# Gate and value products by a 15-product scheme on three token blocks and three weight groups

## The chip, the cores and the metric

One core of a Trainium2 chip runs the whole program in one launch. The metric is device time in microseconds (us), the median of several runs.

## The reference, cut to what matters

Three parts follow one another. All is in float32 (the matrices of the two feed-forward parts come in as 64-bit floats).

```
attn = softmax within chunks of 64 tokens, 8 heads of 64, 8 x 576 tokens   -> x: 4608 x 512
h    = relu(x @ w_in)           w_in 512 x 2048
y    = (h * h) @ w_out          w_out 2048 x 512          -> y: 4608 x 512
gate = sigmoid(y @ w_gate)      w_gate 512 x 1536
val  = y @ w_val                w_val  512 x 1536
out  = (gate * val) @ w2_out    w2_out 1536 x 512
```

The change concerns `gate` and `val`.

## The kernel before, in words

Everything is kept transposed: 128 features on the partitions, tokens along the row. A float32 operand is split into a high and a low part (`split`: ScalarE writes the high part, VectorE subtracts it and writes the low part), and each 128x128 by 128x512 product is three matmuls on TensorE, high by high, low by high, high by low. So one block product over 256 input features is six matmuls.

Four stages follow each other on TensorE. Stage 1 is attention and `x @ w_in`. Stage 2 is `(h*h) @ w_out` (class `Long`, matmuls at L1097). Stage 3 is gate and val (class `Unit`, matmuls at L689). Stage 4 is the last product (class `Long` again). Each of these products uses the Winograd form of Strassen's scheme: a 2 by 2 arrangement of blocks, seven block products in place of eight. In stage 3 the input features make two halves, the weight rows two halves (twelve groups of 128 features, six pairs) and the tokens a pair of blocks of 512. There are nine token blocks, so four pairs, and block 0 is done alone as two halves of 256 columns. A unit is one pair of weight groups of one matrix by one pair of token blocks.

The token blocks of a unit need seven operands, four of them sums (`token_ops`: four subtractions of two blocks each on GpSimd, and fourteen splits). The results need three copies out of PSUM on ScalarE and three additions on VectorE. Then the gate takes four sigmoids on ScalarE, and val four multiplications, three on GpSimd and one on VectorE (`finish2`). The products are stored in DRAM (`ud`) for stage 4.

Weights are prepared during stages 2 and 3. `to_float32` turns a 64-bit block into float32: a load into `wr`, two passes on ScalarE (L526, L530), three on VectorE (L533, L537, L544), one on GpSimd (L551). `weight_group` makes of two such blocks four sums on GpSimd, and splits of 512, 512, 512 and 256 words (`wx`). `through_dram` stores these in DRAM, and before its first use in either half of the stage each weight operand is brought back once and stays in SBUF. Stage 3 goes twice over the tokens, with half of the weights each time.

The order on every engine is written out ahead of time by `Plan`: each operation is a job with a cost and a due time worked out backwards from the TensorE job that needs it. TensorE jobs of the `main` stream run in the order of the code. An engine takes the ready job that is due first, so preparation fills the gaps of VectorE. `look` bounds how long before its due time a job may take SBUF, and `lead` puts a load's due time earlier. The SBUF room is 206 KB a partition. In stage 1 the prepared weights of `w_in` hold eight times 14 KB of it, the token operands 42 KB and the attention output 12 KB. PSUM has eight banks of 128x512.

Of the kernel before, what the change touches and what calls it, by code (L numbers as in the profile page):

```python
# [36 lines left out]


# [336 lines left out]
def tile_attention_relu2_glu(  # L375
# [12 lines left out]
    nc = tc.nc  # L388
# [115 lines left out]
    turn, count = [], [0]  # L504

    def to_float32(src, name, look=None, raws=None):
# [8 lines left out]
        if src.shape[0] == DM:  # L515
            dma(
                lambda: at(raw, None, I32).rearrange("p (c x) -> p c x", c=KD),
                lambda: src.rearrange("(c p) f -> p c f", p=P),
                writes=[raw], size=P * BLK * 8, look=look,
            )  # L520
        else:
            dma(lambda: at(raw, None, I32), lambda: src, writes=[raw], size=P * BLK * 8, look=look)
# [656 lines left out]
    with tc.manual_schedule():  # L1179
# [106 lines left out]
        def blocks_g(s):  # L1286
            def load(r, c):
                got, n = [], W2[s]
                a = A2[s] + c * n
                for kp in range(G1):  # L1290
                    t = sbuf(n, "g")
                    f = r * G1 + kp
                    dma(lambda t=t: at(t), lambda f=f: gd[f][:, a:a + n],
                        [gb[f, b] for b in range(a // BL1, (a + n - 1) // BL1 + 1)], [t], size=P * n * 4, look=13.0)
                    got.append(t)
# [13 lines left out]
        def y_of(m, a, n):  # L1309
# [9 lines left out]
        halves = (range(G2 // 2), range(G2 // 2, G2))  # L1319
        order = [[*PAIRS[:2], (0,), *PAIRS[2:]], [*PAIRS[::-1], (0,)]]  # L1320
        LK = 260.0, 500.0
        back = {(m, g): prepared(w, g, G2, f"{'gv'[m]}{g}", LK[h is halves[1]])
                for h in halves for g in h for m, w in enumerate((wg, wv))}
        back_o = [prepared(w2o, f, G2, f"o{f}", 900.0, rows) for f in range(G2)]
        w2 = {}

        def tokens(s):
            blocks = {}
            for r, c in ((0, 0), (1, 0), (0, 1), (1, 1)):
                if len(s) == 1:  # L1330
                    t = sbuf(BLK, "yr")
                    dma(
                        lambda t=t: at(t).rearrange("p (k c) -> p k c", k=2),
                        lambda r=r, c=c: yd[:, 2 * r:2 * r + 2, c * HB:(c + 1) * HB],
                        y_of(2 * r, c * HB, HB) + y_of(2 * r + 1, c * HB, HB), [t], size=P * BLK * 4, look=30.0,
                    )
                    blocks[r, c] = [(t, 0)]
                    continue
                blocks[r, c] = []
                for kk in range(2):  # L1340
                    t = sbuf(BLK, "yr")
                    dma(
                        lambda t=t: at(t), lambda a=s[c] * BLK, m=2 * r + kk: yd[:, m, a:a + BLK],
                        y_of(2 * r + kk, s[c] * BLK, BLK), [t], size=P * BLK * 4, look=30.0,
                    )
                    blocks[r, c].append((t, 0))
            return token_ops(blocks, BLK)

        ub = {}
        gates = {}  # L1350

        def finish2(s, g, m):
            def finish(u, row, col, t):
                n, f = u.n, g + row * G2
                if m == 0:
                    src = t if t is not None else u.U
                    t = t if t is not None else sbuf(n, "s")
                    copy(u.words(t), [t], u.words(src), [src], n, func=ACTF.Sigmoid, soon=3.0)
                    gates[row, col] = t
                    return  # L1360
                gate = gates.pop((row, col))
                if t is None:
                    binary("DVE", u.words(gate), u.words(gate), u.words(u.U), ALU.mult, n, [gate], [gate, u.U])
                else:
                    binary("POOL", u.words(gate), u.words(t), u.words(gate), ALU.mult, n, [gate], [gate, t], soon=4.0)
                j = s[col] if len(s) == 2 else 0
                d = Buf(name="u")
                ub.setdefault((f, j), []).append(d)
                a = 0 if len(s) == 2 else col * HB
                dma(lambda: ud[f, j][:, a:a + n], lambda: at(gate), [gate], [d], size=P * n * 4, soon=6.0)  # L1370
            return finish

        def unit2(h, s, g, m):
            def make():
                more = None
                if state.get("s") != s:
                    (state["xs"], more), state["s"] = tokens(s), s
                if (m, g) not in w2:
                    w2[m, g] = {kind: load(look=50.0) for kind, load in back[m, g].items()}
                wide = len(s) == 2  # L1380
                return Unit(w2[m, g], state["xs"], BLK if wide else HB, per if wide else per_h,
                            finish2(s, g, m), f"{s}"), more
            return make

        seq = [(h, s, g) for h in range(2) for s in order[h] for g in halves[h]]
        p0, p1 = order[0][:2]
        seq[:6] = [(0, s, g) for s, g in ((p0, 0), (p1, 0), (p1, 1), (p0, 1), (p0, 2), (p1, 2))]
        units([unit2(h, s, g, m) for h, s, g in seq for m in range(2)])


# [3 lines left out]
        def last_blocks(s):  # L1394
            wide = len(s) == 2

            def load(r, c):
                out_ = []
                for kp in range(G2):
# [4 lines left out]
                        ub[f, j], [t], size=P * n * 4, look=30.0)  # L1404
# [90 lines left out]
```

## Time and profile before

| | |
|---|---|
| median of 3 runs | 1601.63 us (1601.32 to 1601.82) |
| the profiled execution, its own time | 1601.8 us |
| its span in the profile | 1600.0 us |
| TensorE busy | 1584.4 us, 99% of the span |
| VectorE, ScalarE, GpSimd busy | 1306.6, 972.0, 530.8 us |
| bytes moved | 333.27 MB, mean 208 GB/s |

The first lines of the profile's page say how much of the span each engine was busy; the chain says through which engine the last instruction was reached. PE is TensorE, PEld its weight load, DVE is VectorE, ACT ScalarE, POOL GpSimd, SP the engine that issues the transfers. The 1.8 us between time and span lie outside the profile's span. TensorE's granted clock is 1.00 of full speed in all slices.

### The profile page before, as it was taken

What the parts mean: (1) busy time and instruction counts of PE and PEld (TensorE: products, weight loads), DVE (VectorE), ACT (ScalarE), POOL (GpSimd) and SP (SyncE); (2) the same over time, 40 slices, a digit from 0 to 9 for tenths busy, and PEclk for the clock granted to TensorE, in tenths of its full rate; (3) what the DMA queues carried; (4) which work ended last, traced back from release to release, by engine and by line L of the source; (5) the groups of instructions that cost most, each with busy time, mean ns of one, the idle gap of its engine ahead of it and who ended that gap; (6) DMA issues with size and microseconds to landing.
All of it is one profiled execution on the core that took longest, in us unless ns stands there. A gap on an engine that the chain in (4) does not pass through costs nothing.

```text
span 1600.0 us, 29686 instructions
## 1 busy us (share of the span) xinstructions
PE 1584.4 (99%) x10209; PEld 1387.7 (87%) x10209; DVE 1306.6 (82%) x2170; ACT 972.0 (61%) x1922; POOL 530.8 (33%) x432
## 2 busy tenths in 40 slices
PE   8999999999999999999999999999999999999999
PEld 6998999999998888899888898888888888888888
DVE  6968878797989998999998797743786748889886
ACT  7986676676876656566665665543565545555554
POOL 2452402021442111111266685643576641000000
PEclk9999999999999999999999999999999999999999
DMA  9965667677884848487787547586447577866562
GB/s 214 275 166 143 155 190 187 175 207 218 267 290 148 276 152 261 155 280 241 255 279 267 183 146 244 186 281 217 168 162 245 196 260 257 250 196 164 150 174 52
DMA packets 381991, 333.27 MB, mean 208 GB/s; under 512 B 231824, under 2 KB 292240, under 8 KB 381840
## 3 DMA queue, kind: packets, MB, share of 16 engines
q1 hardware_dynamic: 381840, 331.38, 67.8%
q8 instruction: 80, 1.31, 0.4%
q14 instruction: 71, 0.58, 0.1%
HBM read 209.13 MB, written 122.16 MB: 207 GB/s over the span
## 4 chain that ended last, share of the span: by engine, by line
PE 92%; DVE 3%; ACT 2%; DMA 1%; SPq 1%; issue 1%; POOL 0%; DVEq 0%; ACTq 0%
PE bank L689 51%; PE bank L1097 37%; SPq L457 1%; PE bank L878 1%; PE bank L940 1%; PE bank L924 1%; PE bank L858 1%; DMA wraw__750<-in_moe_w_in_dram 0%; DMA wf<-wf__3185 0%; PE bank L1077 0%; DMA k__326<-in_k_dram 0%; DVE T__2019 L484 0%; DMA gd<-b__3834 0%; DVE B__760 L484 0%; DMA ql__4671<-in_q_dram 0%
## 5 line engine op out<-in xcount | busy, mean ns | idle before, releaser
L551 POOL TENSOR_TENSOR wf__6958<-wf__6958,wr__6912 128x512 int32<-128x512 int32 x18 | 28.2, 1568 | 163.1 <-DVE wf__6958 L544 119.8
L551 POOL TENSOR_TENSOR wf__3185<-wf__3185,wr__3118 128x512 int32<-128x512 int32 x16 | 21.8, 1361 | 174.0 <-DVE wf__3185 L544 120.1
L551 POOL TENSOR_TENSOR wf__7071<-wf__7071,wr__6912 128x512 int32<-128x512 int32 x18 | 25.4, 1413 | 99.0 <-DVE wf__7071 L544 73.2
L493 POOL TENSOR_TENSOR raw__523<-raw__724,raw__523 128x384 f32<-128x384 f32 x20 | 24.2, 1229 | 30.1 <-DVE B__653 L484 12.3
L530 ACT ACTIVATE wr__6912<-wr__6912 128x512 int32<-128x512 uint32 x36 | 23.9, 665 | 0.0
L484 DVE TENSOR_TENSOR wx__7016<-ws__7143,wx__7016 128x512 fp32r<-128x512 f32 x18 | 17.8, 988 | 6.0 <-ACT wx__7016 L479 6.0
L493 POOL TENSOR_TENSOR ws__7143<-wf__7071 128x256 f32<-128x256 f32 x12 | 12.5, 1038 | 30.5 <-DVE wx__7684 L484 29.9
L484 DVE TENSOR_TENSOR wx__7684<-ws__7143,wx__7684 128x512 fp32r<-128x512 f32 x18 | 17.9, 997 | 4.7 <-ACT wx__7684 L479 4.7
L484 DVE TENSOR_TENSOR wx__7154<-wf__7071,wx__7154 128x256 fp32r<-128x256 f32 x18 | 14.2, 787 | 3.5 <-ACT wx__7154 L479 3.5
L479 ACT ACTIVATE wx__7154<-wf__7071 128x256 fp32r<-128x256 f32 x18 | 7.4, 411 | 15.8 <-POOL wf__7071 L551 15.6
L493 POOL TENSOR_TENSOR ws__7143<-ws__7143,wf__6958 128x256 f32<-128x256 f32 x18 | 16.2, 898 | 1.2
L533 DVE TENSOR_SCALAR wf__7071<-wf__7071 128x512 f32<-128x512 f32 x18 | 11.8, 653 | 5.6 <-ACT wf__7071 L526 5.4
L533 DVE TENSOR_SCALAR wf__6958<-wf__6958 128x512 f32<-128x512 f32 x18 | 10.3, 572 | 6.3 <-ACT wf__6958 L526 6.3
L493 POOL TENSOR_TENSOR ws__7143<-wf__6958,wf__7071 128x256 f32<-128x256 f32 x18 | 15.3, 848 | 0.3
L526 ACT ACTIVATE wf__3185<-wr__3118 128x512 f32<-128x512 f32 x16 | 10.6, 664 | 6.9 <-DMA wf<-wf__3185 6.9
L904 DVE TENSOR_REDUCE mx__379<-bank 128x4 f32<-128x256 f32 x16 | 6.6, 415 | 10.0 <-PE bank L878 10.0
L526 ACT ACTIVATE wf__7071<-wr__6912 128x512 f32<-128x512 f32 x18 | 11.9, 662 | 4.4 <-DMA wr__6912<-in_moe_w_gate_dram 1.9
L544 DVE SCALAR_TENSOR_TENSOR wf__6958<-wr__6912,wf__6958 128x512 int32<-128x512 int32 x18 | 14.1, 781 | 0.2
L533 DVE TENSOR_SCALAR wf__3185<-wf__3185 128x512 f32<-128x512 f32 x16 | 8.1, 506 | 7.5 <-ACT wf__3185 L526 7.5
L544 DVE SCALAR_TENSOR_TENSOR wf__7071<-wr__6912,wf__7071 128x512 int32<-128x512 int32 x18 | 13.8, 766 | 0.3
L526 ACT ACTIVATE wf__6958<-wr__6912 128x512 f32<-128x512 f32 x18 | 11.9, 659 | 3.1 <-DVE wod__6685 L484 1.5
L904 DVE TENSOR_REDUCE mx__2010<-bank 128x4 f32<-128x256 f32 x16 | 6.7, 417 | 8.5 <-PE bank L878 8.5
(5753 smaller groups left out, 6044.5 us busy)
## 6 DMA issues: line engine op xcount, KB each, us to landing
ad<-wx__7016 SPq DMA_DIRECT2D x27, 512.0 KB, 4.1
ad<-wx__7684 SPq DMA_DIRECT2D x27, 512.0 KB, 5.1
wr__3118<-in_moe_w_out_dram SPq DMA_DIRECT2D x16, 512.0 KB, 4.6
wr__6912<-in_moe_w_gate_dram SPq DMA_DIRECT2D x12, 512.0 KB, 4.7
wr__6912<-in_moe_w_val_dram SPq DMA_DIRECT2D x12, 512.0 KB, 4.4
wr__6912<-in_moe_w_out_dram SPq DMA_DIRECT2D x12, 512.0 KB, 3.9
ad<-wx__7154 SPq DMA_DIRECT2D x18, 256.0 KB, 3.7
wf<-wf__3185 SPq DMA_DIRECT2D x16, 256.0 KB, 4.5
```

Source lines behind the costliest of these rows:

```text
L457: nc.sync.dma_start(out=a, in_=b)
L484: lambda: nc.vector.tensor_tensor(out=lo(), in0=at(src, n, F32, off), in1=hi().bitcast(F32), op=ALU.subtract),
L493: eng, cost(eng, n), lambda: e.tensor_tensor(out=o(), in0=a(), in1=b(), op=op),
L526: nc.scalar.activation(out=at(w), in_=t[:, :, 1].bitcast(F32), func=ACTF.Abs)
L530: nc.scalar.activation(out=low, in_=low.bitcast(U32), func=ACTF.Copy, scale=2.0**-29)
L533: nc.vector.tensor_scalar_max(at(w), at(w), TINY)
L544: nc.vector.scalar_tensor_tensor(out=wi, in0=words()[:, :, 1], scalar=-0x40000000, in1=wi, op0=ALU.bitwise_and, op1=ALU.bitwise_or,)
L551: nc.gpsimd.tensor_tensor(out=wi, in0=wi, in1=words()[:, :, 0], op=ALU.add)
L689: nc.tensor.matmul(out=o, lhsT=at(op, P, F32R, wi * size + half * HB + kk * P), rhs=at(xb, n, F32R, xi * xsize + off), start=(first and kk ...
L858: nc.tensor.transpose(out=at(ps, P, F32, hp * P), in_=at(r, P, F32, hp * P), identity=ident)
L878: nc.tensor.matmul(out=o[c][to, hp, :], lhsT=qv[part, hp, tok], rhs=kv[part, hp, tok], start=True, stop=True,)
L1097: nc.tensor.matmul(out=at(ps[m], n), lhsT=at(w, P, F32R, wi * size + half * HB + m * P), rhs=at(x, n, F32R, xi * n), start=(first and kp = ...
```

## The change

- Gate and val use a scheme of 15 block products for a 3 by 2 by 3 arrangement (18 in the plain form): three token blocks of 512 (`THREES`), two halves of the input features, three weight groups of 128 rows (`g`, `g + 4`, `g + 8`). There are three passes over the weights, one for each three token blocks, with four `Group3` in a pass.
- `STEPS` gives the order of the 15 products, the PSUM bank each goes to, and what is done to the banks after it. Gate and val run in step: each product is done for the gate and then for val.
- All sums move to VectorE: 11 token sums (`LEFT_SUMS`), 12 weight sums (`RIGHT_SUMS`), 11 additions of a bank for each matrix, and all nine multiplications of gate by val. GpSimd keeps the last step of `to_float32`, and the sums for `w2_out`.
- The token operands of a three (30 of 4 KB) stay in SBUF for a pass. The weights don't: each product loads its operand, gate and val beside each other (`w3`, 512 KB), from DRAM (`wd3`), so each is loaded in all three passes.
- The buffers of the preparation (26 KB) are taken in one piece by the first load, which has a lead of 260 us and a look of 500. The preparation of `w2_out` follows in the same load buffers, with look 300 and lead 200.
- Many transfers count for 0.7 of their bytes in the planner's own costs. The instructions of stages 1, 2 and 4 stay the same, but for their order.

```
 STEPS = [                 # product, bank, first in the bank, what follows ('c' copy, 'a' add a bank, 'f' finish)
    (13, 2, True, [('c', 'x1', 2, 1)]),
    (6, 0, True, [('a', 'x1', 'x1', 1, 0, -1), ('f', 'o6', 's', 'x1', 1, 0)]),
    (11, 5, True, [('c', 'x2', 5, 1), ('c', 'x3', 5, -1)]),
    (1, 0, False, [('a', 'x2', 'x2', 1, 0, -1)]),
    (3, 0, False, [('a', 'x3', 'x3', 1, 0, 1), ('f', 'o4', 's', 'x3', 1, 0)]),
    (7, 1, True, [('c', 'x4', 1, 1)]),
    (9, 3, True, [('a', 'x2', 'x2', 1, 3, -1), ('f', 'o3', 's', 'x2', 1, 0), ('c', 'x5', 3, -1)]),
    (0, 1, False, [('c', 'x6', 1, -1)]),
    (10, 3, False, [('a', 'x6', 'x6', 1, 3, -1), ('f', 'o2', 's', 'x6', 1, 1)]),
    (14, 1, False, [('a', 'x5', 'x5', 1, 1, -1), ('f', 'o5', 's', 'x5', 1, 0)]),
    (4, 2, False, [('c', 'x7', 2, 1)]),
    (8, 4, True, [('a', 'x6', 'x6', 1, 4, 1)]),
    (12, 2, False, [('a', 'x4', 'x4', 1, 2, -1), ('f', 'o0', 's', 'x4', 1, 0), ('a', 'x6', 'x6', 1, 2, 1), ('f', 'o1', 's', 'x6', 1, 0)]),
    (5, 4, False, [('a', 'x7', 'x7', 1, 4, 1)]),
    (2, 0, False, [('f', 'o7', 'b', 0, 1), ('a', 'x7', 'x7', 1, 0, 1), ('f', 'o8', 's', 'x7', 1, 0)]),
 ]
...
+        def weights3(g, m):
+            src = (wg, wv)[m]
+            have = {}
+            for c in range(3):
+                w = to_float32(columns(src, g + c * G3), f"w{m}", (500.0,500.0,500.0,500.0)[g], (raws3, chunks3))
+                for r in range(2):
+                    have[r * 3 + c] = (w, r * HB)
...
+            for p, *_ in STEPS:
+                v = RIGHT[p]
+                b, off = get(v)
+                op = ops3[0]
+                ops3.append(ops3.pop(0))
+                if p in TURNED:
+                    turned_split(op, b, off)
+                else:
+                    split(op, b, HB, off=off)
+                if sums.used(v) and v >= 6:
+                    free.append(b)
+                dma(lambda p=p: wd3[g, p][:, m * BLK:(m + 1) * BLK], lambda op=op: at(op, None, F32), [op], [wb3[g, p]],
+                    size=P * 8 * HB * 0.7, soon=8.0)
...
+        ahead[0] = 260.0
+        for g in range(G3):
+            for m in range(2):
+                weights3(g, m)
+        taken.extend([*raws2[2], *slots2[BLK], *slots2[HB]])
+        ahead[0] = 200.0
+        back_o = [prepared(w2o, f, G2, f"o{f}", 300.0, rows) for f in range(G2)]
...
+            def run(self):
+                for p, c, first, todo in STEPS:
+                    w = Buf(8 * BLK, name="w3", op=True)
+                    dma(lambda w=w: at(w, None, F32), lambda p=p: wd3[self.g, p], [wb3[self.g, p]], [w],
+                        size=P * 8 * BLK * 0.7, look=15.0)
+                    for m in range(2):
+                        if first:
+                            self.banks[m][c] = psum("M")
+                        product3(self.banks[m][c], w, m, self.xs[p], first)
+                        for step in todo:
+                            self.step(m, step)
...
+        for js in THREES:
+            xs = tokens3(js)
+            for g in range(G3):
+                Group3(js, g, xs).run()
```

## Rows read from the trace of the kernel before

**Rows 1.** The page: busy time of TensorE, and the chain by engine.

```profile
PE 1584.4 (99%) x10209; PEld 1387.7 (87%) x10209; DVE 1306.6 (82%) x2170; ACT 972.0 (61%) x1922; POOL 530.8 (33%) x432
...
PE 92%; DVE 3%; ACT 2%; DMA 1%; SPq 1%; issue 1%; POOL 0%; DVEq 0%; ACTq 0%
```

**Rows 2.** The chain in order of time: start, duration, what, matmuls.

```profile
474.02 345.06 PE bank L1097 x1680
819.08 513.27 PE bank L689 x2484
1337.02 254.44 PE bank L1097 x1224
```

**Rows 3.** Windows of all engines, stages 2 and 3: busy us (instructions), clock, DMA share, GB/s.

```profile
470.00:812.00 342.00, 342.00 (x1673) 290.63 (x1672) 324.56 (x546) 209.60 (x391) 59.66 (x48) 1.00 0.69 226
812.00:1330.00 518.00, 518.00 (x2498) 438.13 (x2497) 367.45 (x474) 283.35 (x534) 312.99 (x235) 1.00 0.63 216
```

**Rows 4.** Windows of all engines: 100 us in stage 2, 100 us in stage 3.

```profile
500.00:600.00 100.00, 100.00 (x443) 82.84 (x442) 97.80 (x157) 60.52 (x103) 11.60 (x8) 1.00 0.54 179
...
1000.00:1100.00 100.00, 100.00 (x443) 82.84 (x442) 52.82 (x75) 45.95 (x82) 48.51 (x39) 1.00 0.70 237
```

**Rows 5.** Windows of L689 where only products of 256 columns run: PE, PEld.

```profile
1310.00:1320.00 10.00, 10.00 (x86) 10.00 (x85) 1.00 0.79 264
1320.00:1330.00 10.00, 10.00 (x85) 10.00 (x85) 1.00 0.80 260
```

**Rows 6.** Timeline of VectorE, end of stage 2: start, duration, instruction.

```profile
776.79 0.68 DVE L484 TENSOR_TENSOR wx__7684<-ws__7143,wx__7684 128x512 fp32r<-128x512 f32 x1
777.39 0.41 DVE L484 TENSOR_TENSOR wx__7154<-wf__7071,wx__7154 128x256 fp32r<-128x256 f32 x1
777.73 0.68 DVE L484 TENSOR_TENSOR x__9212<-g__9227,x__9212 128x512 fp32r<-128x512 f32 x1
778.33 0.68 DVE L484 TENSOR_TENSOR wx__7016<-ws__7143,wx__7016 128x512 fp32r<-128x512 f32 x1
```

**Rows 7.** Groups of instructions by form, VectorE, 440 to 780: busy, mean ns, idle before.

```profile
L544 DVE SCALAR_TENSOR_TENSOR wf__6958<-wr__6912,wf__6958 128x512 int32<-128x512 int32 x6 | 4.1, 687 | 0.1
...
L537 DVE TENSOR_SCALAR wf__6958<-wf__6958 128x512 int32<-128x512 int32 x6 | 2.6, 426 | 0.1
L533 DVE TENSOR_SCALAR wf__7071<-wf__7071 128x512 f32<-128x512 f32 x6 | 2.5, 420 | 0.5 <-ACT wf__7071 L526 0.3
```

**Rows 8.** Windows of GpSimd's L551, stage 2.

```profile
470.00:812.00 342.00, 20.18 (x12) 1.00 0.69 226
```

**Rows 9.** Windows of GpSimd's L493, stage 3.

```profile
812.00:1330.00 518.00, 279.96 (x211) 1.00 0.63 216
```

**Rows 10.** The tile `wr`: its loads, ns min/median/max, first and last start.

```profile
L457 SPq DMA_DIRECT2D wr__6912<-in_moe_w_gate_dram x12: 383/384/483, 523.7 to 1030.0; - x12
L457 SPq DMA_DIRECT2D wr__6912<-in_moe_w_val_dram x12: 383/384/1512, 551.6 to 1055.0; - x12
```

**Rows 11.** Timeline of VectorE, start of stage 3: splits beside a GpSimd subtraction.

```profile
813.06 1.78 DVE L484 TENSOR_TENSOR B__9472<-yr__9336,B__9472 128x512 fp32r<-128x512 f32 x1
814.77 1.77 DVE L484 TENSOR_TENSOR B__9476<-yr__9345,B__9476 128x512 fp32r<-128x512 f32 x1
```

**Rows 12.** Timeline, stage 3: an addition from PSUM, and its wait on TensorE.

```profile
1068.42 0.69 DVE L493 TENSOR_TENSOR b__11795<-b__11795,bank 128x512 f32<-128x512 f32 x1 [0.21 <-PE bank L689]
```

**Rows 13.** Windows of all engines, start of stage 4; the last two numbers are DMA share, GB/s.

```profile
1345.00:1350.00 5.00, 5.00 (x23) 4.14 (x23) 4.93 (x9) 3.39 (x6) 0.00 (x0) 1.00 1.03 417
...
1360.00:1400.00 40.00, 40.00 (x178) 33.14 (x177) 32.53 (x53) 21.52 (x37) 0.00 (x0) 1.00 0.86 250
```

**Rows 14.** Windows of L1097, start of stage 4: the 10 us around the first of these.

```profile
1340.00:1350.00 10.00, 10.00 (x45) 8.28 (x45) 1.00 0.96 350
```

**Rows 15.** Groups of instructions, ScalarE, 812 to 1330.

```profile
L464 ACT ACTIVATE c__11380<-bank 128x512 f32<-128x512 f32 x7 | 4.2, 598 | 14.8 <-PE bank L689 14.8
```

**Rows 16.** The tile `ud`: a store, issue time in ns, first and last start.

```profile
L457 SPq DMA_DIRECT2D ud<-s__9956 x5: 319/319/320, 862.8 to 1006.6; - x5
```

More of the change, by code (lines that the diff above doesn't have):

```diff
@@ L502, in rows @@
         return w[f * P:(f + 1) * P, :]
-    turn, count = [], [0]
+    turn, count, taken, ahead = [], [0], [], [0.0]
     def to_float32(src, name, look=None, raws=None):
@@ new lines, in tile_attention_relu2_glu, with __init__, used @@
+        taken.extend([*raws3[1:], *chunks3, *sums3, *ops3])
+        steps_of = {id: (x, y, {"+": ALU.add, "-": ALU.subtract}[o]) for id, x, y, o in (*LEFT_SUMS,)}
+        sums_of = {id: (x, y, {"+": ALU.add, "-": ALU.subtract}[o]) for id, x, y, o in (*RIGHT_SUMS,)}
+        class Sums:
+            def __init__(self, of, wanted):
+                self.of, self.left = of, {}
+                for v in wanted:
+                    self.left[v] = self.left.get(v, 0) + 1
+                for x, y, _ in of.values():
+                    self.left[x] = self.left.get(x, 0) + 1
+                    self.left[y] = self.left.get(y, 0) + 1
+            def used(self, v):
+                self.left[v] -= 1
+                return not self.left[v]
@@ new lines, in tile_attention_relu2_glu, with product3, go @@
+        ub = {}
+        def product3(ps, w, m, xs, first):
+            def go():
+                o = at(ps, BLK)
+                for kk in range(2):
+                    for i, (wi, xi) in enumerate(((0, 0), (1, 0), (0, 1))):
+                        nc.tensor.matmul(
+                            out=o,
+                            lhsT=at(w, P, F32R, m * BLK + wi * HB + kk * P),
+                            rhs=at(xs[kk], BLK, F32R, xi * BLK),
+                            start=(first and kk == 0 and i == 0),
+                            stop=(kk == 1 and i == 2),
+                            skip_group_check=True,
+                        )
+            job("PE", 6 * per, go, [w, *xs] if first else [w, *xs, ps], [ps], stream="main")
@@ L1355, in finish @@
                 if m == 0:
[L1356 to L1359, printed above, removed]
+                    gate = sbuf(BLK, "s") if kind == "b" or left[0] else t
+                    copy(words(gate), [gate], words(t), [t], BLK, func=ACTF.Sigmoid, soon=3.0, scale=float(sign))
+                    self.gates[name] = gate
@@ L1367, in finish @@
+                f, j = self.g + c * G3, self.js[i]
                 d = Buf(name="u")
                 ub.setdefault((f, j), []).append(d)
[L1369 to L1388, printed above, removed]
+                dma(lambda: ud[f, j], lambda: at(gate), [gate], [d], size=P * BLK * 4 * 0.7, soon=6.0)
+        for js in THREES:
+            xs = tokens3(js)
+            for g in range(G3):
+                Group3(js, g, xs).run()
```

162 lines of the change are left out of this document (119 added, 43 removed), and 15 rows, old and new, of the table STEPS.

## The prediction

> **What bounds the kernel now.** I began with the page: TensorE is busy for 99% of the span, and 92% of the chain that ends last is TensorE's own [rows 1]. The chain in order of time then gives the stages: one unbroken piece of 345 us in stage 2, one of 513 us for gate and val, one of 254 us in stage 4 [rows 2]. No wait interrupts the stage that is changed. Its time is its count of matmuls, so any matmul that goes is time gained, as long as nothing else becomes late.
>
> What could become late is read from the windows. In stage 2 VectorE is busy for 324.6 of 342 us, in stage 3 for 367.5 of 518, the transfers take 0.69 and 0.63 of their engines [rows 3]. So the resource next to TensorE is VectorE, and it is fuller before the changed stage than in it. In a stretch of 100 us TensorE is held up by nothing with VectorE busy for 97.8 [rows 4]: I take that as the share that can be used.
>
> **Matmuls.** A matmul of 512 columns takes 100/443 = 0.2257 us [rows 4], one of 256 columns 20/171 = 0.117 us [rows 5]. Before: 4 pairs x 6 groups x 2 matrices x 7 products x 6 = 2016 wide ones and 6 x 2 x 42 = 504 narrow ones, 455.0 + 59.0 = 514.0 us (the chain shows 513.3 with some records missing [rows 2]). After: 3 passes x 4 groups x 2 x 15 x 6 = 2160 wide ones, 487.5 us. The change removes 26.5 us.
>
> **VectorE's price list.** Back to back, an operation of 512 words starts 0.60 us after the one before it, one of 256 words takes 0.34 (777.39 to 777.73) [rows 6], though the first is shown as 0.68 long. The three steps of a conversion are 0.42, 0.43 and 0.69 [rows 7], the last counted at its pitch of 0.60, so 1.45 us in all. Beside a GpSimd operation a split grew to 1.78 us [rows 11]. How much of that is usual comes from stage 2: 546 operations [rows 3], of which 12 conversions (12 on GpSimd [rows 8]) make 36, some 103 are of 256 words and 407 of 512, cost 17 + 35 + 245 = 297 us by this list; 27.3 us are left over for 48 GpSimd operations, at most 0.57 us each.
>
> **What moves to VectorE.** In a `Group3` each matrix has 11 additions of a bank, and val nine multiplications: 31 operations of 512 words, 18.7 us in the 40.6 us that its 180 matmuls take. A three's tokens need 22 sums and 30 splits, 31.3 us. Preparing gate and val takes, for each of eight units (a group of one matrix), three conversions, 12 sums and 15 splits of 256 words: 4.4 + 9.2 = 13.5 us, and 1.7 for the neighbourhood of its three GpSimd steps, 15.2 us. Over the stage this is a large addition, but GpSimd's 280 us of sums and multiplications [rows 9], which made VectorE's operations long, go with it. Averaged over passes two and three VectorE has 8 x 18.7 + 2 x 31.3 + some 32 for `w2_out` = 244 of 325 us: covered.
>
> **The place where it is late.** Today the g and v blocks are loaded from 523.7 to 1055.0 us [rows 10], because the second half of the weights is needed only in the second half of the stage. After the change the first pass, 162.5 us long, goes through all of them, so the last must be ready by some 122 us after the stage begins. An earlier start finds no room: in stage 1 the weights, token operands and output leave 206 - 112 - 42 - 12 = 40 KB for attention and everything else, and the preparation claims 26 KB at once. I let it start at 470. So VectorE's account is that of 470 to 975, 505 us:
>
> - stage 2's own work: a `Long` unit has 32 subtractions, 56 splits and 6 additions, 94 operations; four wide units 226 us, the narrow one 32, the end of the `w_out` preparation 12: 270
> - four groups of the first pass: 74.6
> - the first three's tokens: 31.3
> - eight units of preparation: 121.6
> - what stands early of the next three's tokens (their operands need the room of the old ones): 8, taken between 0 and 16
>
> Together 505.5 us; at 97.8% that takes 516.9, so TensorE waits 12 us for weights. The ends: with no cost beside GpSimd and no early tokens the account is 484 and nothing waits. With 1.1 us for each of the 24 steps (1.78 less 0.68 [rows 11]) and 16 us of tokens, at the 95% of stage 2's whole window [rows 3], it is 526, and the wait 49 us. I take 12, as the measured surplus and the fullest window are of the same kind of work.
>
> A split beside GpSimd can also wait for the whole GpSimd operation, as those of 1.78 us did [rows 11]; the account's 0.57 says that most don't. The Trainium skill ("SBUF — State Buffer", Who interferes with whom) speaks for the worse case: the engine that comes second on the port pair shared by VectorE and GpSimd is blocked for the other's whole instruction. By the row's 0.57 a conversion step on GpSimd costs VectorE 14 us in 24 steps, by that rule up to 41; the trace agrees for single operations and not for the sum.
>
> **The other costs.** The same bank is read and accumulated again closest at product 1 and then 3: an addition must read it in the 6 x 0.2257 = 1.35 us that the other matrix takes. It needs the 0.21 us hand-over, 0.69 us [rows 12] and as much of a hand-over back, 1.1 us; an operation ahead of it on VectorE may stand in its way. That is 24 places of between 0 and 0.6 us; I take 0.2, so 5 us. At step 9 four banks of each matrix are in use, all eight, but the next is wanted ten products later. ScalarE has 23 operations a group at 0.6 us [rows 15], 14 of 40.6 us: covered. SP issues some 324 loads and stores for the stage itself, at 0.32 us [rows 16] 104 of 487 us; a store that waits for its product holds the weight loads behind it, which are asked for 15 us ahead. The preparation of `w2_out` stands behind that of gate and val on the same buffers, and has passes two and three. Changed weights in the planner's costs change the order only; I give them nothing, between -3 and +3 us.
>
> **Sum.** The profiled execution took 1601.8 us, the median of the runs is 1601.6. 1601.8 - 26.5 + 12 + 5 = 1592 us.
>
> **The rivals.**
>
> First, *the preparation is in time.* VectorE still has room after 812, and GpSimd leaves it alone. Then 1601.8 - 26.5 and 3 for the close places, 1578 us. Against it: stage 2's window is 95% busy already with half the blocks [rows 3].
>
> Second, on the other side, *the transfers bind in the first pass.* VectorE lets (342 x 0.978 - 270 - 10)/15.2 = 3.6 units through by 812, so 4.4 are left, at 3 x 0.524 MB read and 15 x 0.262 MB written: 24 MB. The pass itself reads 60 x 0.524 = 31.5 MB of weights, stores 9.4 and reads 3.1 for the next tokens. 68 MB in 162.5 us is 420 GB/s. The best 10 us show 350 [rows 14], 5 us of them 417, and 40 us of loads of 2 KB rows 250 at a share of 0.86 [rows 13], 291 at a full one. At 350 the pass takes 195 us, 32 longer, and this takes the place of VectorE's 12: 1601.8 - 26.5 + 32 + 5 = 1612 us. It decides against the change from some 22 us on, so from about 370 GB/s down. For it: rate and need are that near. Against it: the more VectorE prepares in stage 2, the less is left. The Trainium skill ("DMA: Bandwidth & Descriptors", Specifications) gives about 358 GB/s as the limit of HBM for a core; by that 190 us, 28 longer, and 1608 us. The 417 of one window stands against it as a strict limit.
>
> Third, *each GpSimd step blocks VectorE for its length.* 24 steps of 20.18/12 = 1.7 us [rows 8] are 41 us in place of 14, the account is 533, the wait 40 us, and the time 1620 us. For it: VectorE would have no gaps into which GpSimd's steps fall. Against it: it had few in stage 2 either.
>
> Fourth, *streaming is short in all three passes.* Later passes need 44 MB and half of `w2_out`'s 17 MB, 53 MB in 162.5 us or 324 GB/s, at 291 some 19 us longer each: 1612 + 38 = 1650 us. Against it: weights come in rows of 4 KB, like those behind the 417 [rows 13].
>
> **Chances.** My forecast, within some 12 us of 1592: 0.40; the preparation in time: 0.20; the first pass bound by transfers: 0.25; GpSimd's steps: 0.07; all passes: 0.08. What a measurement of this kernel can tell from no change is about 0.2%, 3.2 us. Of the forecast's 0.40, 0.33 is faster, 0.06 the same and 0.01 slower; the first rival is faster; of the second 0.05 is the same and 0.20 slower; the other two are slower. So 0.53 faster, 0.11 the same, 0.36 slower. The range is 1576 to 1618: it takes in the first two rivals with some 6 us behind 1612, and leaves out the other two and the worst end of VectorE's account, together under 0.2.
>
> **What would show it.** Right: the gate/val stage holds 2160 wide matmuls, none of 256 columns; TensorE's idle time is some 17 us, nearly all in the first pass, before the third and fourth groups, and ends by a weight load that waited for VectorE or its store; VectorE is over 95% busy from 500 to 975 and near 75% after it; passes two and three have TensorE at 99%. If transfers bind, their share is 1.0 in the first pass while VectorE has gaps. If the waits stand at every 1-then-3, in all passes, the 5 us are too small. The prediction is wrong if TensorE already waits in stage 2, or if the preparation begins far from 470.

## The result, and the profile after

The changed kernel takes 1619.1 us (1617.4 to 1619.9) against 1601.6 us before, a ratio of 1.011 (95% interval 1.009 to 1.013): 17.5 us slower where some 10 us faster was forecast, and 1 us beyond the range. The profiled execution took 1619.6 us. One of the eight executions of e4, below, took 8873 us: it is left out of e4's time, and e4's trace, which is of that execution, isn't used for times.

The page has TensorE busy for 97% of the span, not 99% [rows 1], and VectorE for 85%:

```profile
PE 1572.6 (97%) x9849; PEld 1356.4 (84%) x9849; DVE 1370.9 (85%) x2516; ACT 960.4 (59%) x1920; POOL 248.4 (15%) x214
```

Where the time went is read from TensorE's timeline around the borders of the stages. Stage 2 is L1125 now, gate and val L1474:

```profile
474.72 1.55 PE L1125 MATMUL bank<-x__6399,woa__5720 128*128 128x512 f32 x6
...
839.19 0.84 PE L1474 MATMUL bank<-x__9620,w__9625 128*128 128x512 f32 x3
```

The chain in order of time gives the border to stage 4, and its length:

```profile
1203.50 151.25 PE bank L1474 x666
1354.75 254.41 PE bank L1125 x1224
```

Stage 2, in which no TensorE instruction was changed, takes 364.5 us instead of 345.1 [rows 2]: 19.4 more. Gate and val take 515.6 us; by the pitch of 0.2257 us their 2160 matmuls need 487.5, and the stage before stood 3.9 us above its own 514.0. So 24.2 us of delay are in it. Stage 4 is the same. -26.5 + 19.4 + 24.2 + 0.7 (a later start of stage 2) = 17.8 us, the whole difference of the profiled executions.

TensorE's waits, in stages 2 and 3 of the changed kernel (line, what was waited for, us, times, longest):

```profile
PE bank L1474 <- DMA w__10207<-wd: 11.2, 1, 11.2
PE bank L1125 <- DVE x__7204 L508: 4.3, 2, 2.9
PE bank L1474 <- DVE c__9882 L517: 4.3, 2, 3.3
PE bank L1125 <- DVE x__6617 L508: 2.7, 3, 2.1
PE bank L1474 <- DVE c__10383 L517: 1.9, 1, 1.9
PE bank L1125 <- DVE x__7056 L508: 1.9, 1, 1.9
```

The first is the fourth group's first weight tile. The `c` are the 1-then-3 places (where product 3 waits until VectorE has read its bank after product 1); `x` in L1125 are stage 2's own splits, which VectorE brings late. If each matmul's start is compared with the pitch, the extra over 0.25 us sums to 17 us in stage 2, 8 at the 1-then-3 places of the first pass, 14 at the fourth group, and 2 in small ones: 41 us, against the 17 forecast (12 for weights, 5 for the 1-then-3 places). By pass (PE busy, granted clock, DMA share, GB/s) the delay ends with the first:

```profile
839.00:1002.00 163.00, 145.56 (x620) 0.95 0.88 329
1002.00:1165.00 163.00, 162.07 (x712) 1.00 0.94 342
1165.00:1327.00 162.00, 161.69 (x713) 1.00 0.91 329
```

The stretches of [rows 3] in all engines (PE, PEld, DVE, ACT, POOL), and the first part of stage 2 in pieces:

```profile
470.00:812.00 342.00, 331.06 (x1588) 273.61 (x1587) 320.71 (x615) 204.98 (x412) 40.51 (x22) 1.00 0.69 230
...
500.00:600.00 100.00, 96.45 (x411) 75.78 (x410) 98.67 (x175) 58.74 (x110) 6.96 (x5) 1.00 0.60 199
600.00:700.00 100.00, 97.52 (x417) 78.51 (x416) 92.25 (x171) 58.84 (x115) 15.11 (x6) 0.98 0.69 231
700.00:812.00 112.00, 107.12 (x627) 94.04 (x626) 102.80 (x231) 66.79 (x150) 10.15 (x4) 1.00 0.73 241
```

VectorE does 615 operations instead of 546 in the same 342 us, but is busy for less, 320.7 us: from 600 to 812 us it is idle for 8%, though TensorE waits for it. One such place shows how. ScalarE's and VectorE's timelines:

```profile
775.93 0.62 ACT L503 ACTIVATE x__7204<-g__6705 128x512 fp32r<-128x512 f32 x1
...
778.11 0.69 DVE L508 TENSOR_TENSOR x__7056<-g__6312,x__7056 128x512 fp32r<-128x512 f32 x1
782.08 0.69 DVE L517 TENSOR_TENSOR g__7957<-g__7409,g__7957 128x512 f32<-128x512 f32 x1 [3.28 <-DMA g__7409<-gd]
782.69 0.68 DVE L508 TENSOR_TENSOR x__7204<-g__6705,x__7204 128x512 fp32r<-128x512 f32 x1
```

and TensorE's:

```profile
783.43 0.97 PE L1125 MATMUL bank<-x__7204,wos__6042 128*128 128x512 f32 x3 [2.92 <-DVE x__7204 L508]
```

VectorE takes its operations in the written order. The high part of `x__7204` is ready at 776.55 us, but ahead of its split stands a subtraction whose result is only split from 786 us on, and that waits 3.28 us for a g block (one of stage 2's token blocks) from DRAM. On SP that load (775.32) stood right behind a store of the preparation, before which SP was idle for 1.36 us, so the store can explain less than half of the wait:

```profile
773.11 0.44 SPq L481 DMA_DIRECT2D g__6667<-gd  x1
774.91 0.32 SPq L481 DMA_DIRECT2D wd<-wx__6911  x1
775.32 0.38 SPq L481 DMA_DIRECT2D g__7409<-gd  x1
```

### The profile page after: what moved, and what is told of

The parts are those of the page before. It is cut to its first block, busy times and chain, and to the rows that moved or that the text cites. A ratio compares the mean times of both kernels' runs of the same rounds, so it can differ in the third digit from the quotient of the medians.

```text
span 1617.8 us, 29417 instructions
## 1 busy us (share of the span) xinstructions
PE 1572.6 (97%) x9849; PEld 1356.4 (84%) x9849; DVE 1370.9 (85%) x2516; ACT 960.4 (59%) x1920; POOL 248.4 (15%) x214
## 3 DMA queue, kind: packets, MB, share of 16 engines
q8 instruction: 78, 1.28, 0.3%
## 5 line engine op out<-in xcount | busy, mean ns | idle before, releaser
L579 POOL TENSOR_TENSOR wf__6664<-wf__6664,wr__6620 128x512 int32<-128x512 int32 x10 | 19.4, 1937 | 208.8 <-DVE wf__6664 L572 146.1
L579 POOL TENSOR_TENSOR wf__3197<-wf__3197,wr__3130 128x512 int32<-128x512 int32 x16 | 21.2, 1323 | 178.3 <-DVE wf__3197 L572 125.9
L517 DVE TENSOR_TENSOR c__9882<-c__9882,bank 128x512 f32<-128x512 f32 x38 | 26.0, 684 | 15.4 <-PE bank L1474 7.3
L579 POOL TENSOR_TENSOR wf__6900<-wf__6900,wr__5457 128x512 int32<-128x512 int32 x10 | 15.9, 1586 | 126.8 <-DVE wf__6900 L572 116.8
L517 POOL TENSOR_TENSOR raw__535<-raw__736,raw__535 128x384 f32<-128x384 f32 x20 | 24.2, 1228 | 30.2 <-DVE B__665 L508 12.7
L579 POOL TENSOR_TENSOR wf__6683<-wf__6683,wr__6620 128x512 int32<-128x512 int32 x4 | 8.9, 2216 | 121.6 <-DVE wf__6683 L572 58.8
L488 ACT ACTIVATE c__9882<-bank 128x512 f32<-128x512 f32 x22 | 13.1, 597 | 12.6 <-PE bank L1474 5.0
L579 POOL TENSOR_TENSOR wf__6900<-wf__6900,wr__6620 128x512 int32<-128x512 int32 x4 | 6.7, 1664 | 77.3 <-issue 74.9
L579 POOL TENSOR_TENSOR wf__6664<-wf__6664,wr__5457 128x512 int32<-128x512 int32 x4 | 6.1, 1518 | 76.1 <-DVE wf__6664 L572 76.1
L488 ACT ACTIVATE c__9882<-c__9882 128x512 f32<-128x512 f32 x14 | 8.8, 632 | 11.6 <-DVE c__9882 L517 11.6
L579 POOL TENSOR_TENSOR wf__6683<-wf__6683,wr__5457 128x512 int32<-128x512 int32 x4 | 8.5, 2133 | 46.9 <-DMA wd<-wx__6926 22.1
L517 DVE TENSOR_TENSOR c__12520<-c__12520,bank 128x512 f32<-128x512 f32 x16 | 10.9, 684 | 5.2 <-PE bank L1474 4.0
L554 ACT ACTIVATE wf__3197<-wr__3130 128x512 f32<-128x512 f32 x16 | 10.6, 662 | 6.5 <-DMA wf<-wf__3197 6.5
L561 DVE TENSOR_SCALAR wf__3197<-wf__3197 128x512 f32<-128x512 f32 x16 | 7.6, 476 | 7.8 <-ACT wf__3197 L554 7.8
L1474 PE MATMUL bank<-x__9620,w__10207 128*128 128x512 f32 x6 | 3.1, 656 | 11.2 <-DMA w__10207<-wd 11.2
L986 ACT ACTIVATE raw__535<-bank 128x256 f32<-128x256 f32 x36 | 12.1, 382 | 2.9 <-PE bank L968 2.6
L986 ACT ACTIVATE raw__736<-bank 128x256 f32<-128x256 f32 x36 | 11.7, 393 | 2.2 <-PE bank L968 2.1
L517 POOL TENSOR_TENSOR raw__535<-raw__535 128x384 f32<-128x384 f32 x10 | 12.8, 1296 | 0.0
```

The costliest lines, as they stand in the source:

```text
L488: lambda: nc.scalar.activation(out=o(), in_=i(), func=func, **kw), ib, ob, soon=soon,
L517: eng, cost(eng, n), lambda: e.tensor_tensor(out=o(), in0=a(), in1=b(), op=op),
L554: nc.scalar.activation(out=at(w), in_=t[:, :, 1].bitcast(F32), func=ACTF.Abs)
L561: nc.vector.tensor_scalar_max(at(w), at(w), TINY)
L579: nc.gpsimd.tensor_tensor(out=wi, in0=wi, in1=words()[:, :, 0], op=ALU.add)
L986: nc.scalar.activation(out=o[:, :, a:a + CH], in_=i, func=ACTF.Copy)
```

## Experiments

"Gains" are against the changed kernel's 1619.1 us, ratios are to the kernel before. The first four keep the changed kernel's written order on every engine.

**e1 and e2: less work for VectorE.**

```
-  binary("DVE", word(v), a, b, op, HB, [o[0]], reads)     # 96 sums
+  (nothing; the splits read a raw block)                  # e1
+  and the 120 low parts written by ScalarE copies         # e2
```

> The changed kernel in its own order on every engine, with the 96 sums of the gate and val weights left out (each operand is split from the raw block with which its sum begins, so the output differs). VectorE is relieved of 96 x 0.34 = 33 us before and in the first pass; transfers and matmuls stay. VectorE theory: TensorE's 41 us of waits (17 in stage 2, 24 in the gate/val stage) shrink by 20 to 33 us, time 1587 to 1599. Transfer theory: at most 5 us, 1614 or more. GpSimd theory: at most 8 us, since 24 blocking steps stay.

> As the run without sums, and the 120 low parts of the weights written by ScalarE as plain copies (output differs): VectorE keeps only the conversions, 73 us less. VectorE theory: nearly all of the 41 us go, also those of stage 2; 1578 to 1588. Transfer theory: 1612 or more. GpSimd theory: 1610 or more.

e1: 1603.1 us, ratio 1.001 (1.000 to 1.002), a gain of 16. e2: 1601.9 us, 1.001 (1.000 to 1.002), 1.2 more. No theory had these times: the gain is 4 and 14 us short of what the VectorE theory asked for, and more than the other two allow. Stage 2's extra time fell from 17 to 5 or 6 us; the wait before the fourth group stayed, 11.0 and 10.6 us. VectorE's throughput is part of it, but in this order more than 33 us of relief brings hardly anything (e2 also gives ScalarE 120 operations more).

**e3: half of each weight load.**

```
-  dma(... at(w, None, F32), lambda p=p: wd3[self.g, p] ...
+  dma(... at(w, BLK, F32),  lambda p=p: wd3[self.g, p][:, :BLK] ...
```

> The changed kernel in its own order, with each weight tile loaded by half (256 of 512 KB; gate and val are multiplied by the same half, so the output differs): 47 MB less to read, 16 MB of it in the first pass. VectorE theory: at most 6 us faster, 1613 or more, stage 2 unchanged. Transfer theory: most of the gate/val stage's 24 us go, about 1598; stage 2 keeps its 17 us.

1613.3 us, 1.008 (1.006 to 1.010), as the VectorE theory had it. 47 MB less gave 6 us; the wait at the fourth group is still 9.9. The transfers aren't the main thing that holds TensorE.

**e4: GpSimd's step (`five`, L579) of the 24 conversions on 32 of 512 columns.**

```
-  nc.gpsimd.tensor_tensor(out=wi, in0=wi, in1=words()[:, :, 0], op=ALU.add)
+  nc.gpsimd.tensor_tensor(out=wi[:, :32], in0=wi[:, :32], in1=words()[:, :32, 0], op=ALU.add)
```

> The changed kernel in its own order, with GpSimd's step of each gate and val weight conversion done on 32 of 512 columns (output differs), so that it holds VectorE up for a short time only. Theory of GpSimd's blocking: 25 us or more faster, 1594 or less. VectorE theory: 24 steps of at most 1.1 us each shift at most 14 us, 1605 to 1615. Transfer theory: no change.

1606.3 us, 1.003 (1.002 to 1.004): 12.8 us for 24 steps, 0.53 us each. A time alone could hide more, as e1's 33 us of relief gave only 16. But the changed kernel's own timeline has the same price: from 470 to 999 us, 16 of the 24 conversion steps on GpSimd run beside VectorE operations that are longer than the median of their form, by 12.7 us in all, so 0.53 us a step. That is near the 0.57 of the prediction's account, and not the 1.7 of the third rival.

**e5 and e11: e1 with a new written order; e11 meant to have e4's short step as well.**

```
   while v >= 6: v = sums_of[v][0]      # e5: planned without the sums
   job("POOL", 0.2, five, ...)          # e11: and with a short step (in the planner's costs alone)
```

> The 96 right-hand sums of the weights are left out as in e1 (the products read a raw block), but here the program's planner also writes a new order for all engines, with the shorter preparation. Theory 'order' (the wait of 11 us before the fourth group's first weights, and most of the rest, come from how far down VectorE's, ScalarE's and SP's fixed queues the preparation's steps were written, so that fewer instructions in the same order can't move them): the wait before the fourth group goes, TensorE's idle time beside its matmul pitch falls from 41 us to under 12, and the time is 1578 to 1590. Theory 'way there' (the wait is the length of the chain from the last conversion over sum, split, store and load, whatever the order): the wait stays at 10 to 12 us and the time is 1598 to 1606, as in e1.

> As e5 (a new order, and the 96 right-hand sums left out, the products reading raw blocks), and the GpSimd step of gate's and val's conversions on 32 of its 512 columns. Theory 'room': the GpSimd steps cost VectorE little, and the time is that of e5, 1589 to 1595. Theory 'blocking': the rest of e5's 14 us of extra time goes with them, and the time is 1580 to 1587, near that with a single group prepared (e6).

e5: 1592.8 us, 0.995 (0.994 to 0.997), 3 us beyond what "order" expected. The wait at the fourth group is gone, and 14 us of extra time are left.

e11: 1610.6 us, 1.005 (1.004 to 1.007). It doesn't test what its expectation says. The kernel asks which conversions are meant only when their instructions are written, after planning, and by then the mark that singles out gate's and val's has been taken back; only the cost told to the planner took effect. In the trace all of e11's GpSimd steps are on 512 columns. So e1, e5 and e11 hold the same instructions (VectorE 2420, GpSimd 214) in three orders, and take 1603.1, 1592.8 and 1610.6 us. Order alone is worth 18 us, and that e5 beats e1 by 10 needn't come from planning without the sums. e11's last store of prepared weights leaves at 930.9 us, e5's at 970.4, but stage 2 takes 377 us in e11 and 354 in e5: here the preparation that was done earlier was paid for by stage 2.

**e6: only the first group's weights prepared, used for all four.**

```
-  for g in range(G3):                        +  for g in range(1):
-  lambda p=p: wd3[self.g, p]                 +  lambda p=p: wd3[0, p]
-  ahead[0] = 260.0                           +  ahead[0] = 200.0
```

> Only the first weight group's 30 operand tiles are prepared (2 units of 8), and all four groups' products read these; the preparation is planned 200 us ahead instead of 260. So the arithmetic on gate and val, the number of products, their loads and the combining of the results are as in the changed kernel, and three quarters of the preparation are away. Theory 'preparation' (all that the change loses lies in getting the weights ready in time; the 15 products themselves give what their count says): gate and val take 487 to 493 us, stage 2 is back at 345 to 347, the time is 1574 to 1582. Theory 'scheme' (the 15 products with their 1-then-3 combining or their streamed loads hold TensorE also when nothing is late): gate and val stay at 500 us or more, the time is 1588 or more.

1584.9 us, 0.990 (0.988 to 0.991). Gate and val take 492.6 us (826.7 to 1319.3), of which 2.4 are extra time at 1-then-3 places; stage 2 takes 353.0. The longest waits left are stage 2's splits:

```profile
PE bank L1125 <- DVE x__6504 L508: 1.9, 1, 1.9
PE bank L1125 <- DVE x__7054 L508: 1.8, 1, 1.8
PE bank L1125 <- DVE x__9245 L508: 0.9, 1, 0.9
```

So the scheme gives what its count says once the weights are there, and three quarters of the preparation, together with the order that goes with them, cost 34 us. The time is 3 us over what "preparation" expected: the quarter left still costs stage 2 some 7 us.

**e7: planned 200 us ahead.** `ahead[0] = 200.0`.

> The preparation is planned 200 us ahead instead of 260, nothing left out. Theory 'order' (VectorE, ScalarE and GpSimd together have too little free time before the first pass ends, so a later start only moves the waits): TensorE's extra time in stage 2 falls from 17 us to under 6, that in the first pass of gate and val rises from 24 to over 32 us, and the time is 1612 to 1628. Theory 'crowding' (the preparation loses time because it is squeezed in among stage 2's own steps, and would be ready in time without that): stage 2 falls to under 6 us as well, the first pass stays at 24 or less, and the time is 1598 to 1608.

1627.8 us, 1.017 (1.015 to 1.019). Extra time: 12 us in stage 2 ("order" expected under 6), 38 in gate and val. A later start doesn't free stage 2 in proportion, and the first pass loses more: "crowding" falls.

**e8: groups 3 and 4 wanted later.**

```
-  for js in THREES: ... for g in range(G3)
+  for i, gs in ((0, (0, 1)), (1, (0, 1, 2, 3)), (0, (2, 3)), (2, (0, 1, 2, 3))):
-  ahead[0] = 260.0
+  ahead[0] = 300.0
```

> Nothing is left out. The order of the groups is changed: the first three token blocks with weight groups 1 and 2, then the second three with groups 1 to 4, then the first three with groups 3 and 4, then the last three with all; preparation planned 300 us ahead. Groups 3 and 4 of the weights are first wanted after four groups of products instead of two and three, so some 82 us later. Theory 'order' (what is missing is free time of the engines before the weights are wanted): the waits at groups 3 and 4 go, those of stage 2 stay (10 to 20 us) because the start is earlier, and the time is 1595 to 1608. Theory 'way there' (the first load after each unit's last store waits for its chain): a wait of 8 us or more stands again before groups 3 or 4, and the time is 1612 or more.

1617.3 us, 1.010 (1.009 to 1.012). No group waits for its weights any more, but stage 2 takes 374 us, 29 more than before the change. The "order" theory has the mechanism and too small a price; "way there" has the time for a wrong reason. As the first three token blocks are gone through twice, their operands are also made twice, which is 52 VectorE operations more than in the changed kernel.

**e9, e15, e10, e16: the GpSimd step meant to go to VectorE, planned 260, 275, 290 and 300 us ahead.**

```
-  nc.gpsimd.tensor_tensor(..., op=ALU.add)          # 24 conversions of gate and val
+  nc.vector.tensor_tensor(..., op=ALU.bitwise_or)
-  ahead[0] = 260.0                                  +  ahead[0] = 275.0 | 290.0 | 300.0
```

> The GpSimd step of gate's and val's conversions (24 additions of the low bits) becomes a bitwise 'or' on VectorE; so that no carry is needed, ScalarE's step before it scales the low word by 0.93 more, which changes at most the last bit of the float32. A new order is planned, nothing else changes. Theory 'room' (a GpSimd step costs VectorE about 0.57 us, as the prediction counted, so that 0.60 us of VectorE's own time is no better): VectorE is as short as before, TensorE's extra time stays at 35 to 45 us, the time is 1612 to 1624. Theory 'blocking' (a GpSimd step of 1.9 us holds VectorE, or what waits for the step, for nearly its length): 24 x 1.3 us = 31 us come back at most, TensorE's extra time falls under 25 us, and the time is 1588 to 1604.

> As e9, with the preparation planned 290 us ahead instead of 260. Theory 'blocking': with GpSimd out of the preparation an earlier start takes up the rest of stage 2's room, and the time is at most that of e9, 1584 to 1602, perhaps under that of the kernel before. Theory 'room': VectorE is full in stage 2 whatever the start, the waits move from the first pass of gate and val into stage 2, and the time is 1612 to 1630.

> As e9 and e10 (the GpSimd step of gate's and val's conversions done by VectorE), with the preparation planned 275 us ahead. Theory 'start' (an earlier start lets VectorE do more of the preparation while TensorE is held by nothing): the time lies between those of 260 and 290 us ahead, 1606 to 1616. Theory 'order' (each written order has its own waits, whatever the start): outside that, by more than 3 us on either side.

> As e15, planned 300 us ahead. Theory 'start': 1596 to 1604, at or below e10's 1604. Theory 'order' or a start too early (the preparation takes room from attention and from stage 2's operands): 1608 or more.

1617.9 us (ratio 1.010, 1.007 to 1.012), 1612.7 (1.007, 1.005 to 1.008), 1604.3 (1.002, 1.001 to 1.003) and 1652.8 (1.032, 1.030 to 1.034).

None of the four moved the step. As in e11, the mark was taken back (`raws3_of[0] = None`) before the instructions were written, so the planner placed the step as 0.61 us of VectorE, and the program still gave it to GpSimd, on 512 columns. In e10, 214 GpSimd and 2516 VectorE operations are the changed kernel's counts, and L583 on POOL (GpSimd) is the step:

```profile
PE 1566.4 (98%) x9849; PEld 1351.0 (84%) x9849; DVE 1373.2 (86%) x2516; ACT 959.1 (60%) x1920; POOL 248.2 (15%) x214
...
L583 POOL TENSOR_TENSOR wf__6526<-wf__6526,wr__6330 128x512 int32<-128x512 int32 x4 | 9.1, 2273 | 70.6 <-DVE wf__6526 L573 60.0
...
L583 POOL TENSOR_TENSOR wf__6696<-wf__6696,wr__6330 128x512 int32<-128x512 int32 x4 | 9.9, 2467 | 47.6 <-DVE wf__6696 L573 47.6
```

So "room" and "blocking" stay untested here, and what e9 would have cost on VectorE isn't known. What the four are, with e7, is the changed kernel's instructions in other written orders. That makes them a test of the order alone. e10 is the best version that leaves nothing out: 14.8 us better than the changed kernel without one instruction less, and still 3 us behind the kernel before (its ten executions lie between 1599.6 and 1610.5). From e7 to e10 the time falls as VectorE's first step of the preparation comes earlier (table). Each is a single order, so the start isn't shown to be the reason. In e16 that step comes at 462.5 us, 7 us before e10's, and the time is 48 us longer: TensorE is busy 104 of 125 us at the start of stage 2, where it waits for its operands. Why is open. (e15 has the time of its "start", e16 that of its "order"; e10 lies between its two theories.)

The instructions being the same, VectorE's work from 470 us to the last store of prepared weights is nearly the same too, and the time follows the share of that stretch in which it is busy. The share is work over length, so it restates how late the last store is; it is no second cause. The windows of the changed kernel and of e10 are:

```profile
470.00:999.00 529.00, 488.16 (x932) 0.98 0.76 266
```

```profile
470.00:985.00 515.00, 491.45 (x929) 1.00 0.78 273
```

| kernel | VectorE's first step of the preparation, us | VectorE busy, to the last store | share | time |
|---|---|---|---|---|
| e7, 200 ahead | 553.5 | 491.2 of 538 | 0.913 | 1627.8 |
| changed kernel, 260 | 517.5 | 488.2 of 529 | 0.923 | 1619.1 |
| e9, 260 | 517.5 | 489.0 of 532 | 0.919 | 1617.9 |
| e15, 275 | 480.2 | 485.8 of 519 | 0.936 | 1612.7 |
| e10, 290 | 469.3 | 491.5 of 515 | 0.954 | 1604.3 |

**e12, e13, e14: the preparation's transfers out of SP's queue.** SP's waits showed up to 13.5 us for a GpSimd step of the preparation, and the load above stood behind one of its stores. e12 issues the 120 stores from GpSimd, e13 the 24 loads too, e14 is e10 with both.

```
-  nc.sync.dma_start(out=a, in_=b)
+  nc.gpsimd.dma_start(out=a, in_=b)      # preparation of gate and val only
```

> The 120 stores of gate's and val's prepared tiles are issued by GpSimd instead of SP, each at its old place in the written order; nothing else is changed or left out. Theory 'SP's queue' (in stage 2 a store that waits on SP for a preparation split holds the loads of stage 2's own blocks that stand behind it, VectorE then waits for such a block, and the split that TensorE wants stands behind it on VectorE): VectorE's waits for loads of g blocks from 600 to 812 us fall from 9 us to under 3, stage 2 gets 5 to 12 us shorter than 364.5, and the time is 1605 to 1614. Theory 'VectorE' (it is simply full): stage 2 stays at 362 to 367, the time at 1616 to 1622. If GpSimd, waiting for the splits, holds its own conversion steps behind the stores, preparation gets later and the wait before the fourth group grows over 11 us.

> As e12, and the 24 loads of gate's and val's raw blocks are issued by GpSimd too, which wait for a buffer that a GpSimd step frees (SP waited up to 13.5 us for such a step). Theory 'SP's queue': no transfer of the preparation stands ahead of one that TensorE's own work needs any more; stage 2 is 346 to 355 us, and the time is 1598 to 1609. Theory 'VectorE': 1614 to 1622.

> e10 (the GpSimd step of gate's and val's conversions done by VectorE, preparation planned 290 us ahead) with the preparation's stores and loads issued by GpSimd as in e13, where nothing but these issues is left of the preparation on GpSimd. Theory 'SP's queue': stage 2's 20 us and the first pass's 6 us of extra time in e10 go down to 15 in all, and the time is 1588 to 1597, below the kernel before. Theory 'VectorE': 1600 to 1608, as e10.

e12: 1617.1 us, 1.010 (1.008 to 1.011); e13: 1622.0, 1.014 (1.012 to 1.016); e14: 1618.1, 1.010 (1.009 to 1.012), 14 us worse than e10. In e12 stage 2 does get 5.4 us shorter, and VectorE's waits for g blocks from 600 to 812 us fall from 9.6 to 6.2, but gate and val take 1.8 us more, and the time is only 2 us better. The theory of SP's queue falls as the main cause; it explains single waits. e12 and e13 have the times of "VectorE". e14 holds e13's instructions in an order planned as e10's: the conversion steps are still on GpSimd, and share its queue with the transfers. Both theories missed its time, and why it is 14 us worse than e10 isn't shown.

## Why the prediction went wrong

*Matmuls: right.* Nothing of 256 columns is left, and e6 shows 492.6 us for the stage, 2.4 of them waits: 490.2 for the 2160 matmuls, 2.7 more than forecast.

*The limit and its work: right.* VectorE's account of the preparation was made from 470 to 975 us, 505.5 us of work with all of the fourth group. Up to the last store, at 999, less than half of that group's 18.7 us is in, so some 494 were forecast; 488.2 were measured.

*The failed step: "I take that as the share that can be used", 97.8%.* It came from one stretch of 100 us [rows 4]. The changed kernel reaches as much in such a stretch (98.67 from 500 to 600 us, above), but over the whole of the preparation it used 92.3%, where the prediction's sign of being right was over 95%. With that share the prediction's own formula gives 505.5/0.923 - 505 = 43 us of waiting for weights instead of 12; 33 were measured, beside 8 at the 1-then-3 places. The agreement is no proof, since the share was taken from the kernel that waits. What shows the step wrong is that the same instructions reach 91 to 95%, depending on the written order, and none of these orders reaches 97.8. The stage-2 window [rows 3], 95%, near the best of them, was only taken for the range's end; there, with the dearest GpSimd steps, the prediction had 49 us of waiting, and left them outside its range.

*The place: wrong.* "Nearly all in the first pass, before the third and fourth groups" was forecast, and that the prediction fails "if TensorE already waits in stage 2, or if the preparation begins far from 470". Both happened: VectorE's first step of the preparation stands at 517.5 us, and 17 us of the 41 are in stage 2. The account added up work as if VectorE could do it in any order. The order is written, and where the next operation in it waits, a split that TensorE wants waits with it.

*The 1-then-3 places: size.* 5 us over all passes were forecast. While VectorE was full they cost 8 in the first pass alone; in e6, with VectorE freer, 2.4 in all.

*The fourth group.* The chain that ends in its wait is the last unit of the preparation itself, step after step on four engines:

```profile
972.35 1.10 POOL wf__6683 L579
973.45 0.02 issue
973.48 1.50 DVE ws__6915 L517
974.98 0.02 issue
975.00 0.43 ACT wx__6926 L503
...
976.31 5.83 DMA w__10207<-wd
...
982.18 1.22 PE bank L1474 x2
```

It stays in e1 and goes in e5, which has e1's instructions; it goes in e10, which has the changed kernel's. So the place of these steps in the order sets it, not only their number.

*The rivals.* "In time" needs three quarters of the preparation gone (e6). "Transfers bind" falls by e3 and by passes two and three, where their share is 0.94 and 0.91 (1.00 from 1140 to 1180 us) and TensorE hardly waits. "Each GpSimd step blocks VectorE for its length" named 1620 us, the time that came: that is luck, as e4 and the timeline price a step at 0.53 us. "Short in all passes" isn't seen.

*What stays open* is by what rule an order gets VectorE to 92% or to 95%. In the changed kernel its waits between 518 and 999 us are for g blocks (10.3 us), for ScalarE's high parts (13.7 with the weights' own), and for TensorE's results (5.1), partly a consequence of TensorE's standing still. In e10, from 470 to 985 us, the same three are 2.7, 5.5 and 3.2. So the better order is one in which fewer operations come up before their inputs, but no run changed one of these waits alone, and no order of these instructions was found that beats the kernel before.

## What to carry to other kernels

Where a change hands much work to a nearly full in-order engine, use for its free time the busy share of a long stretch of the same kind of work, not that of a full short one: at 500 us of work each per cent was worth over 5 us. Look for the delay at once in the stage from whose gaps the work is taken, as its own operations now stand behind the new ones.

Where a program writes its order anew for each version, the order is part of the change. Here the same instructions took 1604 to 1653 us in six orders, and e1's took 1593 to 1611 in three. A difference of that size between two newly planned versions says little by itself of what was left out or moved; a version that keeps the old order (e1 to e4) says more. And count the instructions of each engine in the trace before reading a time: 214 on GpSimd, unchanged, say that e9, e10, e15 and e16 moved none.

## What had not been expected of the hardware

- TensorE is slow after a wait. After the 11.2 us without a matmul the granted clock from 982 to 987 us was 0.52, near the lower of its two levels (1.2 of 2.4 GHz), and three matmuls took 1.28 us instead of 0.68. After the 3.3 us at 853.66 it was 0.66 for 5 us. It added about 2 us to each of the two waits:

```profile
853.00:858.00 5.00, 4.34 (x12) 0.66 0.30 120
982.00:987.00 5.00, 4.82 (x12) 0.52 1.02 393
987.00:990.00 3.00, 3.00 (x15) 1.00 1.05 413
```

- A VectorE operation beside a GpSimd step grew to 1.77 us in stage 2 too, here from 525.36 on, while L579 ran from 524.29 to 526.57 us:

```profile
525.36 1.77 DVE L508 TENSOR_TENSOR x__6654<-g__6729,x__6654 128x512 fp32r<-128x512 f32 x1
```

  The Trainium skill ("SBUF — State Buffer", Who interferes with whom) has such an operation wait for the other's whole instruction. This one agrees: it ends 0.56 us after the GpSimd step, near the 0.60 us that such an operation takes by itself. The mean price is far lower, 0.53 us for a step of some 2.0 us: 8 of the 24 steps lengthen no VectorE operation.
- The transfers moved 384 GB/s over 41 us of the first pass (894 to 935 us) and up to 416 in slices of 4 us (the view of the transfers from 835 to 1000 us, in 40 slices):

```profile
GB/s 341 71 367 147 258 26 293 202 121 237 207 359 369 407 409 405 402 399 351 264 383 414 415 398 411 409 404 400 415 406 399 327 253 207 259 370 401 416 411 402
```

  The 358 GB/s that the prediction cites from the Trainium skill ("DMA: Bandwidth & Descriptors", Specifications) are no limit here. The Trainium skill itself says in another place ("Perfetto Trace Analysis", Roofline) that a core can draw more while it is the only active one; that agrees.
- GpSimd takes 0.54 us to issue a store that SP issues in 0.32. The stores of one buffer in e12 (issue time in ns, min/median/max, first and last start):

```profile
L481 POOL DMA_DIRECT2D wd<-wx__6882 x24: 539/542/709, 525.0 to 987.5; - x24
```
